# Attention and feed-forward on one core: the ordered list of the work is made by another procedure

## Chip, core and metric

The kernel runs on one core of one Trainium2 chip. The metric is the device time of one execution in microseconds. Before the change the median of 3 runs is 855.63 us (854.58 to 859.22).

## What is computed

```python
# attention: q, k, v are 8 x 8 x 576 x 64 (batch, heads, positions, head size)
scores = scale * np.matmul(q, k.transpose(0, 1, 3, 2))
rel = pos[:, None] - pos[None, :]
mask = (rel >= 0) & (rel < 64)
scores = np.where(mask, scores, -1000000000.0)
scores = scores - np.max(scores, axis=-1, keepdims=True)
attn = np.exp(scores)
attn = attn / (np.sum(attn, axis=-1, keepdims=True) + 1e-09)
x = np.matmul(attn, v)            # then to 4608 tokens x 512
# feed-forward: w_in 512 x 2048, w_out 2048 x 512
h = x @ w_in
out = np.maximum(0.01 * h, h) @ w_out
```

Each position sees itself and the 63 before it. Everything is float32.

## The kernel before, in words

*Units.* The 576 positions of each batch are cut into blocks of 64. A unit is one block with all 8 heads, and two units are a **pair**; there are 36 pairs, 0 to 35. For each pair the scores go to two PSUM banks (S, L284), come to SBUF with the mask (E, `shield_of`, L694, on VectorE; from pair 20 on `copy_of`, L700, on ScalarE), GpSimd takes the maximum over partitions (P, `max_of`, L709), VectorE subtracts it (B, `minus_of`, L716), ScalarE takes the exponent (X, L720), GpSimd sums over partitions (A, `add_of`, L712), and the values follow on TensorE (V, `values_of`, L768). The sums go through four small DMAs and a reciprocal (L723, L731, L744, L756) before `product_of` (L780, VectorE) scales the values. Pairs 0 to 7 belong to a part that is written out by hand.

*Split weights and x.* A float32 product is made of three matmuls: each operand is split into a high half (a rounded copy, by ScalarE) and a low half (what is left, by VectorE: a subtraction). `prep_low` (called `low` before, L1079), `low_of` (L975), the low half of x (`x_low`, L932) and `wide_low` (L1204) are such low halves.

*Four spans of work on TensorE.* (1) A start written out by hand (the string ORDER) up to about 126 us. (2) The first 1536 tokens: 32 steps of a list called `walk`. A step has 12 matmuls of the first layer (`h`, L955) into a PSUM bank, then ScalarE's `leak` (L969) and `high_of` (L972), then `low_of` (L975) on VectorE, and two steps later 12 matmuls of the second layer (`acc`, L964). Two banks, tags o and h, take the first layer's products in turn. (3) Three further stages of 1024 tokens each, with fewer products by sums and differences of blocks: `m` (first layer, L1155) and either `y` (L1175, in the first of the three) or `z` (L1218, in the last two). Their x comes back from DRAM through `x_build` (differences L910, low halves L932), their weights in sums prepared beforehand (`prepare`, L1050: differences `join_of` L1073, low half L1079), and they are loaded by GpSimd's DMA queue (L1139). `combine` (L1207) makes sums of the activations. (4) The attention of pairs 8 to 35 is woven into spans 2 and 3: a **visit** is the scores or the values of one pair between two of TensorE's large products.

*What sets the order.* From the start of span 2, each operation is entered in a list, `plan`, by `op` (L539): its engine, an estimated duration `us`, its predecessors, a rank, a lag after its predecessors, and for DMAs the time to landing. `arrange` (L551) goes through time: it takes the engine that can begin first, and among the operations that are ready there the one of least rank (numbers written out by hand, such as 0.1 for `low_of`, 0.35 or 1.3 for attention). The order so made is the order of each engine's queue. The estimates know nothing of what one engine does to another. TensorE's large products are one fixed chain (`next_main`, L645); only the visits can move in it. The values of pairs 8 to 19 go into the bank of the first layer that is idle at that moment, so they wait for `low_of` of the product before, and the next product waits for their copy (`take_of`, L775). The scores of pairs 10 to 19 and the values of pairs 8 to 19 (`place="guest"`) may stand only behind a first-layer piece or another guest.

Of the kernel before, what the change touches and what calls it, by code (L numbers as in the profile page):

```python
# [4 lines left out]

# [1 line left out]

# [32 lines left out]
LANES = 8  # L40
# [55 lines left out]

HUGE = float(np.array(0x47EFFE00, np.uint32).view(np.float32))
REBIAS = 2.0 ** -112


def flat(t):
# [4 lines left out]
def band_attention_ffn(ctx: ExitStack, tc: tile.TileContext, qk, vW, vL, w_in, w_out, eye_mask, out, outT):  # L106
# [83 lines left out]
    wi, wo, both = [], [], []  # L190
# [68 lines left out]
    xs = {}  # L259
# [196 lines left out]
    acc, sums, due = {}, {}, []  # L456
# [74 lines left out]
    order, late = ORDER.split("|")  # L531
# [19 lines left out]
    def arrange():  # L551
        free, left = dict.fromkeys(("PE", "DVE", "ACT", "POOL", "SP"), 0.0), list(plan)
        waiting = {e: [] for e in free}
        missing, users = {}, {}
        for x in plan:
            missing[x["n"]] = len(x["after"])
            for a in x["after"]:
                users.setdefault(a["n"], []).append(x)
            if not x["after"]:
                waiting[x["engine"]].append((0.0, x))  # L560
        order, landed, last_place = [], [0.0] * LANES, None

        def fits(x):
            return x["place"] != "guest" or last_place in ("host", "guest")

        def begins(ready, x):
            return max(ready, landed[0]) if x["land"] and x["engine"] != "POOL" else ready

        while any(waiting.values()):
            best = None  # L570
            for e, xs in waiting.items():
                if xs:
                    t = max(free[e], min(begins(*y) for y in xs))
                    if best is None or t < best[0]:
                        best = t, e
            t, e = best
            ready_now = [y for y in waiting[e] if begins(*y) <= t]
            r, x = min([y for y in ready_now if fits(y[1])] or ready_now, key=lambda y: (y[1]["rank"], y[1]["n"]))
            if e == "PE":
                last_place = x["place"]  # L580
                if "bank" in x:
                    for y in [y for y in plan if y.get("opens") and "end" not in y][:1]:
                        y["after"].append(x["bank"])
                        missing[y["n"]] += 1
                        users.setdefault(x["bank"]["n"], []).append(y)
            waiting[e] = [y for y in waiting[e] if y[1] is not x]
            free[e] = t + x["us"]
            x["end"] = free[e] + x["land"]
            if x["land"] and e != "POOL":
                landed.pop(0)  # L590
                landed.append(x["end"])
            order.append(x)
            for y in users.get(x["n"], ()):
                missing[y["n"]] -= 1
                if not missing[y["n"]]:
                    at = max(a["end"] + (0.0 if a["engine"] == y["engine"] and not a["land"] else y["lag"]) for a in y["after"])
                    waiting[y["engine"]].append((at, y))
        assert len(order) == len(plan)
        return order

    MM, TWO, ONE, ACTS = 0.2267, 1.05, 0.72, 0.62

    RING, held = 4, {}
# [49 lines left out]
    for name in late.split():  # L653
        kind = name.rstrip("0123456789")
        n = int(name[len(kind) :])
# [4 lines left out]
        engine, us = ("ACT", ACTS) if kind in ("abs", "chi") else ("DVE", ONE)  # L660
# [7 lines left out]
    ready = {f: [weights_of.get(2 * f + i, {}).get("rest") for i in range(2)] for f in range(FT)}  # L668
# [128 lines left out]
    at, summing = {}, []  # L797
# [88 lines left out]

    def x_build(s, n, xt_of, xt_free, x_free):

        STEP, WIDTH = (0.42, 0.27) if s == 2 else (0.5, 0.35)
# [37 lines left out]
        done = []  # L927
        for a, b, after in ((0, 2, got), (2, 3, got), (3, 7, [d, d2, d3, d4])):
            hi = op("ACT", 0.2 + 0.213 * (b - a), lambda a=a, b=b: nc.scalar.copy(x_view(0, a, b), source(a, b)), *after, *x_free, rank=urge, lag=wait)

            def low(a=a, b=b):
                nc.vector.tensor_tensor(x_view(1, a, b), source(a, b), x_view(0, a, b).bitcast(F32), ALU.subtract)  # L932

            done.append(op("DVE", STEP - 0.27 + WIDTH * (b - a), low, hi, rank=urge))
        return done


# [112 lines left out]
    def prepare(n, f, at, hurry, *freed):  # L1050
# [24 lines left out]
        def high():  # L1075
            nc.scalar.copy(prep(0).bitcast(F32R), prep(1))

        def low():
            nc.vector.tensor_tensor(prep(1).bitcast(F32R), prep(1), prep(0), ALU.subtract)  # L1079

        def keep(i):
# [16 lines left out]
        lo = op("DVE", 1.4, low, hi, rank=hurry)  # L1098
# [365 lines left out]
```

## Time and profile before

| what | us |
|---|---|
| median of 3 runs | 855.63 |
| the profiled execution | 856.94 |
| its span on the core | 855.2 |
| TensorE busy in it | 840.5 |
| VectorE / ScalarE / GpSimd busy | 600.4 / 390.6 / 384.0 |

The profile names engines PE (TensorE), DVE (VectorE), ACT (ScalarE), POOL (GpSimd) and SP (SyncE). In a timeline each row has the start, the length, the engine, the line, the operation with its output and inputs, and how many instructions are merged; a bracket at its end gives the idle time of that engine just before, and what ended it. An engine that is idle but not waited for costs nothing, so the rows of TensorE with a bracket are the ones to look for.

### The profile page before, as it was taken

The page shows a single profiled execution, that of the slowest core. Times are in us where ns is not written, and L with a number is a line of the kernel's source. Part 1 is how long each engine was busy: PE and PEld are TensorE (multiplying, and loading weights), DVE is VectorE, ACT ScalarE, POOL GpSimd, SP SyncE. Part 2 cuts the span into 40 slices and gives each one's busy share as a digit, 9 for nine tenths or more (in the row PEclk, how much of TensorE's full clock was granted, in tenths as well). Part 3 has the DMA queues.
Part 4 walks back from the last instruction along what each step waited for, and adds up shares of the span by engine and source line. Part 5 has one row for each costly group of instructions (what it writes and reads, how often), then busy time and mean ns, then how long its engine had stood idle before and what let it go on. Part 6 is the DMA issues. An engine that isn't in the chain of part 4 may idle for free.

```text
span 855.2 us, 16825 instructions
## 1 busy us (share of the span) xinstructions
PE 840.5 (98%) x6778; PEld 686.8 (80%) x6778; DVE 600.4 (70%) x851; ACT 390.6 (46%) x637; POOL 384.0 (45%) x218
## 2 busy tenths in 40 slices
PE   8999999998999999999999999999999999999998
PEld 5787888886887878888888788878888888888886
DVE  7999885545678678656658996487579955546863
ACT  4666555342334365455555443444365423334431
POOL 5322001777777555776787668656111111111110
PEclk9999999999999999999999999999999999999999
DMA  9884856887889859999999999999988986677682
GB/s 330 264 239 145 266 167 231 284 285 231 268 266 356 294 193 293 298 341 311 316 354 337 372 363 337 378 291 258 303 225 240 246 244 199 197 195 194 192 211 94
DMA packets 143117, 226.80 MB, mean 265 GB/s; under 512 B 15552, under 2 KB 66880, under 8 KB 143040
## 3 DMA queue, kind: packets, MB, share of 16 engines
q0 software_dynamic: 51552, 90.18, 37.9%
q10 hardware_dynamic: 51024, 77.31, 27.9%
q1 hardware_dynamic: 40464, 58.24, 21.4%
q8 instruction: 53, 0.87, 0.4%
q14 instruction: 24, 0.20, 0.1%
HBM read 172.52 MB, written 53.06 MB: 264 GB/s over the span
## 4 chain that ended last, share of the span: by engine, by line
PE 84%; DVE 6%; DMA 5%; issue 2%; ACT 1%; POOL 1%; SPq 0%; ACTq 0%; DVEq 0%; POOLq 0%
PE m L1155 26%; PE z L1218 18%; PE y L1175 10%; PE acc L964 6%; PE h L955 6%; PE h L438 5%; PE acc L474 5%; PE s L284 3%; PE o L768 3%; DMA x_rows<-late_n 1%; DMA p<-x_rows 1%; PE o L374 1%; POOL late_o L712 1%; DMA raw<-w_out 1%; DMA late_r<-rows 1%
## 5 line engine op out<-in xcount | busy, mean ns | idle before, releaser
L1155 PE MATMUL m<-pfew,p 128*128 128x512 f32 x720 | 168.6, 390 | 0.6 <-DVE pxa L1164 0.6
L1155 PEld LDWEIGHTS m<-pfew,p 128*128 128x128 f32 x720 | 134.8, 188 | 29.1 <-DVE pxa L1164 1.0
L1164 DVE TENSOR_TENSOR p<-m,pxa 128x512 f32<-128x512 f32 x60 | 41.3, 690 | 54.2 <-PE m L1155 52.1
L964 PE MATMUL acc<-p,gs 128*128 128x512 f32 x324 | 79.1, 393 | 0.0
L1139 POOL DMA_DIRECT2D p<-w_first x42 | 31.7, 755 | 96.6 <-PE m L1155 62.3
L1167 ACT ACTIVATE p<-p 128x512 f32<-128x512 f32 x60 | 37.6, 630 | 80.4 <-DVE p L1164 80.4
L712 POOL PARTITION_ALL_REDUCE late_o<-late_f x20 | 65.6, 3301 | 14.1 <-ACT late_f L720 8.9
L1164 DVE TENSOR_TENSOR pxa<-m,pxa 128x512 f32<-128x512 f32 x60 | 41.4, 690 | 43.2 <-PE m L1155 42.5
L1155 PE MATMUL m<-pxb,p 128*128 128x512 f32 x288 | 71.2, 393 | 0.3 <-ACT p L1167 0.3
L709 POOL PARTITION_ALL_REDUCE g<-late_f x20 | 37.2, 1907 | 75.7 <-DVE late_f L694 73.4
L712 POOL PARTITION_ALL_REDUCE late_o<-late_e x18 | 60.2, 3367 | 23.7 <-issue 18.4
L964 PEld LDWEIGHTS acc<-p,gs 128*128 128x128 f32 x324 | 60.1, 188 | 13.1
L712 POOL PARTITION_ALL_REDUCE late_o<-e x18 | 58.7, 3287 | 26.4 <-ACT e L720 12.8
L1155 PEld LDWEIGHTS m<-pxb,p 128*128 128x128 f32 x288 | 53.4, 188 | 12.6 <-ACT p L1167 0.7
L1218 PE MATMUL z<-gs,p 128*128 128x512 f32 x240 | 57.6, 389 | 0.0
L955 PE MATMUL h<-pxa,p 128*128 128x512 f32 x228 | 55.6, 391 | 0.2 <-ACT late_n L775 0.2
L1218 PEld LDWEIGHTS z<-gs,p 128*128 128x128 f32 x240 | 45.1, 188 | 9.3
L1139 POOL DMA_DIRECT2D p<-w_second x28 | 22.7, 810 | 66.1 <-PE z L1218 37.0
L1218 PE MATMUL z<-third,p 128*128 128x512 f32 x216 | 51.9, 389 | 0.0
L1218 PE MATMUL z<-pxa,p 128*128 128x512 f32 x216 | 51.9, 389 | 0.0
L955 PEld LDWEIGHTS h<-pxa,p 128*128 128x128 f32 x228 | 42.5, 188 | 9.5 <-ACT late_n L775 0.6
L975 DVE TENSOR_TENSOR gs<-h,gs 128x512 fp32r<-128x512 f32 x32 | 22.0, 687 | 38.7 <-ACT gs L972 38.7
(193 smaller groups left out, 1760.6 us busy)
## 6 DMA issues: line engine op xcount, KB each, us to landing
p<-w_first POOLq DMA_DIRECT2D x42, 1024.0 KB, 7.2
p<-w_second POOLq DMA_DIRECT2D x28, 1024.0 KB, 9.3
p<-w_sums POOLq DMA_DIRECT2D x16, 1024.0 KB, 5.6
qk<-qk ACTq DMA_DIRECT2D x26, 512.0 KB, 5.9
pspare<-w_second ACTq DMA_DIRECT2D x16, 512.0 KB, 8.7
w_sums<-pspare ACTq DMA_DIRECT2D x16, 512.0 KB, 6.3
raw<-w_out ACTq DMA_DIRECT2D x15, 512.0 KB, 4.4
raw<-w_in ACTq DMA_DIRECT2D x14, 512.0 KB, 4.0
```

Source lines behind the costliest of these rows:

```text
L438: nc.tensor.matmul(ps, a[:, k, :], b[:, k, part], start=n == 0, stop=n == len(terms) - 1)
L474: nc.tensor.matmul(acc[c, i], a[:, ts], b, start=begin and n == 0, stop=end and n == 2)
L709: nc.gpsimd.partition_all_reduce(most_of(j), e_of(m)[:, j], P, ReduceOp.max)
L712: nc.gpsimd.partition_all_reduce(sum_of(j), e_of(m)[:, j], P, ReduceOp.add)
L955: nc.tensor.matmul(ps, a[:, k, :], b[:, k], start=i == 0, stop=i == len(terms) - 1)
L964: nc.tensor.matmul(acc[c, i], a[:, i * P : (i + 1) * P], b, start=begin and k == 0, stop=n in ends and k == 2)
L1139: nc.gpsimd.dma_start(to, of, max_dma_last_dim=2048)
L1155: nc.tensor.matmul(tiles[b], w[:, 256 * i + 128 * kt : 256 * i + 128 * kt + 128], x_part(OF_X[k], j, kt), start=begin and c == 0, stop=c = ...
L1164: nc.vector.tensor_tensor(to(), tiles[b], x(), ALU.add)
L1167: nc.scalar.activation(to(), to() if b is None else tiles[b], AF.Prelu, alpha=0.01)
L1175: nc.tensor.matmul(tiles[i], a, b, start=f == 0 and k == 0, stop=f == FT - 1 and k == 2)
L1218: nc.tensor.matmul(tiles[b + i], a, x, start=begin and f == 0 and c == 0, stop=f == half - 1 and c == 2, skip_group_check=not begin,)
```

## The change

`arrange` goes, and `arranged` takes its place. What the operations compute stays, and so do the chain of TensorE's products and the bank for the values of pairs 8 to 19. The new procedure has five parts.

- `measure` replaces the estimated durations and times to landing with measured ones, and marks each operation of VectorE that has two inputs in SBUF (`both`) and each reduction of GpSimd (`reduce`).
- `forward` goes through time as `arrange` did, but by a key that is handed to it. A visit to TensorE is put off until it is due, or joins one that has just run. `port_rule` makes an operation with two inputs in SBUF that would begin during a reduction wait until 0.9 us (maximum) or 1.12 us (sum) before the reduction's end.
- `latest` goes backward from TensorE's chain and gives each operation the latest time at which it can begin.
- `candidates` does both 7 times for each of 3 x 6 pairs of a reserve for DMAs and a lead of the visits, with the latest times as the key.
- `walked` goes through each candidate in order with random delays, and the candidate with the earliest end of TensorE is taken.

```diff
+SLACKS = (1.5, 2.0, 2.5)
+AHEAD = (6.0, 8.0, 10.0, 12.0, 15.0, 20.0)
+ROUNDS = 7
+WALKS = 4
+NOISE = 0.05
+STRETCH = 1.1
+ENTER, LEAVE, SIGNAL = 0.12, 0.2, 0.07
+BOTH_SBUF = {
+    "wide_low": 1.22, "combine": 1.22, "whole_of": 1.22, "prep_low": 1.22, "sub": 0.38, "join_of": 0.41, "x_low": None,
...
+def port_rule(x, t, port, held):
+    end = t + x["us"]
+    if x["both"]:
+        held = end = (port[1] if port[0] <= t < port[1] else t) + x["us"]
+    if x["reduce"]:
+        end = max(t, held) + x["us"]
+        port = end - x["us"], end - (0.9 if x["name"] == "max_of" else 1.12)
+    return end, port, held
...
+    def pe_key(x, t):
+        if due is None or not x["visit"]:
+            return x["rank"] if due is None else 1.0
+        return 0.5 if before or due[x["n"]] <= t else 2.0
...
+def candidates(plan):
+    for dma in SLACKS:
+        slack = dict(dma=dma, POOL=POOL_SLACK, other=0.1)
+        for early in AHEAD:
+            order, hosted = forward(plan, {x["n"]: x["rank"] for x in plan}, slack)
+            for n in range(ROUNDS):
+                late = latest(order, hosted, slack)
+                due = early and {x: t - early for x, t in late.items()}
+                order, hosted = forward(plan, late, slack, due)
+                yield order, hosted
+
+
+def arranged(plan):
+    measure(plan)
+    best = None
+    for order, hosted in candidates(plan):
+        mean = sum(walked(order, hosted, NOISE, STRETCH, i) for i in range(WALKS)) / WALKS
+        if best is None or mean < best[0]:
+            best = mean, order
+    return best[1]
...
-    for x in arrange():
+    for x in arranged(plan):
         x["fn"]()
```

(The rest renames `low` to `x_low` and `prep_low`, so that `measure` can tell them apart.) The new code stands ahead, so the line numbers behind `arrange` grow by 185: L975 becomes L1160, L1079 becomes L1264, L1073 becomes L1258, L780 becomes L965, L768 becomes L953.

What moves is seen in the engines' queues. First VectorE's, around the `low_of` (third row from the end, `gs1_82<-h1_10`) that the values of pair 10 wait for. `pspare` is a tile of weights in preparation, `late_n` values to be scaled, `pxa` the x of the third block of tokens, `late_c` the sums, `s12` the scores of pair 12. Before:

```order
L795 TENSOR_TENSOR pxa1_21_2193<-late_n_1764,pxa0_20_2192 128x4x128
L716 TENSOR_TENSOR late_f_1763<-late_f_1763,g_80 128x512
L694 SCALAR_TENSOR_TENSOR e_76<-s12_0_2199,away_75 128x512
L731 RECIPROCAL late_c0_1768<-late_c0_1768 128x8
L694 SCALAR_TENSOR_TENSOR e_76<-s12_1_2200,away_75 128x512
L1079 TENSOR_TENSOR pspare_18_1777<-pspare_18_1777 128x4x256
L975 TENSOR_TENSOR gs1_82<-h1_10_2174,gs1_82 128x512
L780 TENSOR_TENSOR late_n_1764<-late_n_1764,late_r_1765 128x4x2x64
L795 TENSOR_TENSOR pxa1_21_2193<-late_n_1764,pxa0_20_2192 128x4x128
```

The same place in the queue after the change:

```order
L980 TENSOR_TENSOR pxa1_21_2193<-late_n_1763,pxa0_20_2192 128x4x128
L1258 TENSOR_TENSOR pspare_18_1759<-pspare_18_1759 128x256 x2
L916 RECIPROCAL late_c0_1767<-late_c0_1767 128x8
L1264 TENSOR_TENSOR pspare_18_1759<-pspare_18_1759 128x4x256
L1160 TENSOR_TENSOR gs1_82<-h1_10_2172,gs1_82 128x512
L879 SCALAR_TENSOR_TENSOR e_76<-s12_0_2236,away_75 128x512
L879 SCALAR_TENSOR_TENSOR e_76<-s12_1_2237,away_75 128x512
```

The low half of the weights still stands right ahead of `low_of`, but pair 12's scores are read behind it now, and pair 11's subtraction (`late_f`) has gone from this place.

Second, VectorE's queue around the `low_of` of step h2_6, for which the values of pair 18 wait. `p14` and `p15` are weights in preparation, `pxb` x for the next stage. Before:

```order
L1073 TENSOR_TENSOR p14_24_2914<-p14_24_2914 128x256
L975 TENSOR_TENSOR gs0_81<-h2_5_3294,gs0_81 128x512
L731 RECIPROCAL late_c0_1768<-late_c0_1768 128x8
L1073 TENSOR_TENSOR p14_24_2914<-p14_24_2914 128x256 x3
L1079 TENSOR_TENSOR p14_24_2914<-p14_24_2914 128x4x256
L975 TENSOR_TENSOR gs1_82<-h2_6_3333,gs1_82 128x512
```

After:

```order
L1258 TENSOR_TENSOR p15_23_2844<-p15_23_2844 128x256
L1160 TENSOR_TENSOR gs0_81<-h2_5_3288,gs0_81 128x512
L916 RECIPROCAL late_c0_1767<-late_c0_1767 128x8
L965 TENSOR_TENSOR late_n_1763<-late_n_1763,late_r_1764 128x4x2x64
L1160 TENSOR_TENSOR gs1_82<-h2_6_3329,gs1_82 128x512
L1117 TENSOR_TENSOR pxb_27_3374<-p12_25_3049,pxb_27_3374 128x2x256
L1258 TENSOR_TENSOR p14_24_2959<-p14_24_2959 128x256
```

Between the two `low_of` the weights' preparation is gone and the scaling of a pair's values (`product_of`) is there instead.

Third, TensorE's queue around the values of pair 15 (`o15`); `s17` are scores, `h2_0` and `h2_1` first-layer products. Before:

```order
L284 MATMUL s17_1_2917<-qk1_84 64x64
L768 MATMUL o15_2950<-e_76,more_v_73 64x64 x16
L955 MATMUL h2_0_2904<-pxa0_20_2192,pfew_3_85 128x512
L955 MATMUL h2_0_2904<-pxa1_21_2193,pfew_3_85 128x512
L955 MATMUL h2_0_2904<-pxa0_20_2192,pfew_3_85 128x512 x2
```

After:

```order
L1149 MATMUL acc2_3_2829<-p13_15_1545,gs1_82 128x512 x3
L1140 MATMUL h2_1_2977<-pxa0_20_2192,pfew_3_85 128x512
L1140 MATMUL h2_1_2977<-pxa1_21_2193,pfew_3_85 128x512
L1140 MATMUL h2_1_2977<-pxa0_20_2192,pfew_3_85 128x512 x2
L1140 MATMUL h2_1_2977<-pxa1_21_2193,pfew_3_85 128x512
L1140 MATMUL h2_1_2977<-pxa0_20_2192,pfew_3_85 128x512
L953 MATMUL o15_2991<-e_76,more_v_73 64x64 x16
```

The values stood behind scores; now they stand alone, behind half of a first-layer product, one step later in the walk.

More of the change, by code (lines that the diff above doesn't have):

```diff
@@ new lines, in gap, with visiting @@
+def gap(a, x, slack):
+    if a["land"]:
+        return SIGNAL + slack["dma"]
+    if a["engine"] == x["engine"]:
+        return 0.0
+    return SIGNAL + slack.get(a["engine"], slack["other"])
+def visiting(x, before):
+    return x["us"] + (ENTER if x["visit"] and not before else LEAVE if before and not x["visit"] else 0.0)
+def port_rule(x, t, port, held):
+    end = t + x["us"]
+    if x["both"]:
+        held = end = (port[1] if port[0] <= t < port[1] else t) + x["us"]
[3 more added lines that the diff above has]
+    return end, port, held
@@ new lines, in latest @@
+def latest(order, hosted, slack):
+    late, pinned, t, before = {}, {}, 0.0, False
+    for x in order:
+        if x["engine"] == "PE":
+            if not x["visit"]:
+                pinned[x["n"]] = t
+            t += visiting(x, before)
+            before = x["visit"]
+    taken = {e: ([], []) for e in ("DVE", "ACT", "POOL", "SP")}
+    for x in sorted(order, key=lambda x: x["land"] - x["end"]):
+        ends = [late[y["n"]] - gap(x, y, slack) - x["land"] for y in users_of(x, hosted)]
+        if x["n"] in pinned:
+            ends.append(pinned[x["n"]] + x["us"])
+        end = min(ends, default=t + 20.0)
+        if x["engine"] != "PE":
+            begins, stops = taken[x["engine"]]
+            i = bisect_left(begins, end)
+            while i and stops[i - 1] > end - x["us"] + 1e-9 and begins[i - 1] < end - 1e-9:
+                i -= 1
+                end = min(end, begins[i])
+            i = bisect_left(begins, end - x["us"])
+            begins.insert(i, end - x["us"])
+            stops.insert(i, end)
+        late[x["n"]] = end - x["us"]
+    return late
@@ new lines, in walked, with start @@
+def walked(order, hosted, noise=0.0, stretch=1.0, seed=0):
+    r = Random(seed)
+    queues = {}
+    for x in order:
+        queues.setdefault(x["engine"], []).append(x)
+    at, free = dict.fromkeys(queues, 0), dict.fromkeys(queues, 0.0)
+    done, missing = {}, {x["n"]: len(after_of(x, hosted)) for x in order}
+    port, held, before = (0.0, 0.0), 0.0, False
+    head = {}
+    def start(e):
+        if at[e] == len(queues[e]):
+            return None
+        x = queues[e][at[e]]
+        if missing[x["n"]]:
+            return None
+        t = free[e]
+        for a in after_of(x, hosted):
+            t = max(t, done[a["n"]] + (0.0 if a["engine"] == e and not a["land"] else SIGNAL))
+        return t
+    head = {e: start(e) for e in queues}
+    for _ in order:
+        e = min((e for e in head if head[e] is not None), key=lambda e: head[e])
+        t, x = head[e], queues[e][at[e]]
+        y = x if e == "PE" else {**x, "us": x["us"] * (1 + noise * abs(r.gauss(0, 1)))}
+        end = t + y["us"]
+        if e == "PE":
+            end, before = t + visiting(y, before), x["visit"]
+        elif x["both"] or x["reduce"]:
+            end, port, held = port_rule(y, t, port, held)
+        free[e] = end
+        done[x["n"]] = end + (x["land"] * stretch * (1 + 2 * noise * abs(r.gauss(0, 1))) if x["land"] else 0.0)
+        at[e] += 1
+        touched = {e}
+        for y in users_of(x, hosted):
+            missing[y["n"]] -= 1
+            if not missing[y["n"]]:
+                touched.add(y["engine"])
+        for e in touched:
+            head[e] = start(e)
+    return free["PE"]
@@ L548, in bulk @@
         return op("ACT", 0.5, fn, *after, rank=rank, lag=lag, land=land)
[L551 to L599, printed above, removed]
     MM, TWO, ONE, ACTS = 0.2267, 1.05, 0.72, 0.62
```

103 lines of the change are left out of this document (98 added, 5 removed).

## The prediction

> **What bounds the kernel now.** I read the page's busy shares first. TensorE is the engine that sets the time; the other engines matter only where TensorE waits for them.
>
> ```profile
> span 855.2 us, 16825 instructions
> PE 840.5 (98%) x6778; PEld 686.8 (80%) x6778; DVE 600.4 (70%) x851; ACT 390.6 (46%) x637; POOL 384.0 (45%) x218
> ```
>
> The two numbers differ by 14.7 us. That is the first bound: an order of the same instructions can win little more than this. To see where it lies I went through the timeline of TensorE alone, stretch by stretch, and kept the rows with idle time ahead of them (in brackets, with what ended it). Up to 126 us the order is written out by hand and the change leaves it alone, so only later rows count; the last row is from the view by windows (length, busy time of five engines with instruction counts, granted clock, share and rate of the DMA).
>
> ```profile
> 199.07 1.80 PE L768 MATMUL o<-late_e,v 128*64 128x64 f32 x32 [3.69 <-DVE gs L975]
> 200.80 2.54 PE L955 MATMUL h<-pxb,p 128*128 128x512 f32 x6
> ...
> 262.92 1.15 PE L768 MATMUL o<-e,more_v 128*64 128x64 f32 x32 [1.21 <-DVE gs L975]
> ...
> 308.73 1.15 PE L768 MATMUL o<-e,v 128*64 128x64 f32 x32 [1.00 <-DVE gs L975]
> ...
> 484.56 2.98 PE L1175 MATMUL y<-gs,p 128*128 128x512 f32 x12 [0.57 <-issue]
> ...
> 560.63 1.65 PE L1155 MATMUL m<-pxb,p 128*128 128x512 f32 x6 [0.27 <-ACT p L1167]
> ...
> 568.32 1.65 PE L1155 MATMUL m<-pfew,p 128*128 128x512 f32 x6 [0.57 <-DVE pxa L1164]
> ...
> 190.00:205.00 15.00, 11.31 (x129) 9.25 (x129) 8.81 (x11) 4.13 (x8) 10.14 (x5) 0.89 0.75 250
> ```
>
> The idle times add up to 3.69 + 1.21 + 1.00 + 0.57 + 0.27 + 0.57 = 7.3 us. The first has a second price: behind it the values of pair 10 take 1.80 us and half a product 2.54 us, and the granted clock of that window is 0.89. From the chain of waits (start, length, what) come the same things undisturbed, and the price of a visit of attention to TensorE.
>
> ```profile
> 151.18 1.09 PE s L284 x64
> 152.27 2.95 PE acc L964 x12
> 155.22 2.72 PE h L955 x12
> ...
> 387.74 1.08 PE o L768 x32
> ...
> 421.33 2.02 PE o L768 x64
> ...
> 592.72 30.15 PE m L1155 x132
> ...
> 775.18 76.17 PE z L1218 x336
> ```
>
> Twelve large matmuls take 2.72 us (0.227 each), 2.95 right behind a visit, so entering and leaving costs 0.23 us a group of visits. Values take 1.08 us, two sets in a row 2.02. So pair 10's slow clock cost (1.80 - 1.08) + (2.54 - 1.36 - 0.23) = 1.7 us, of which I count 1.6, since rows of the timeline overlap slightly. Together 7.3 + 1.6 = 8.9 us is what the present order loses at places I can name. From 592 us on there is nothing to win: 132 products in 30.15 us are 0.228 each, 336 in 76.17 us are 0.227.
>
> All three long waits are the values waiting for `low_of` (L975), since they go into the idle first-layer bank, which `low_of` reads last. Why it was late, from the timelines of VectorE and GpSimd:
>
> ```profile
> 195.09 3.23 POOL L712 PARTITION_ALL_REDUCE late_o<-late_f  x1 [1.94 <-DVE late_c L731]
> 195.46 2.96 DVE L1079 TENSOR_TENSOR pspare<-pspare 128x1024 fp32r<-128x1024 f32 x1
> 198.34 0.68 DVE L975 TENSOR_TENSOR gs<-h,gs 128x512 fp32r<-128x512 f32 x1
> ...
> 254.82 6.76 POOL L712 PARTITION_ALL_REDUCE late_o<-late_e  x2 [0.62 <-ACT late_e L720]
> 258.77 2.90 DVE L1079 TENSOR_TENSOR pspare<-pspare 128x1024 fp32r<-128x1024 f32 x1 [1.00 <-ACT pspare L1076]
> 261.59 0.68 DVE L780 TENSOR_TENSOR late_n<-late_n,late_r 128x512 f32<-128x512 f32 x1
> 262.19 0.68 DVE L975 TENSOR_TENSOR gs<-h,gs 128x512 fp32r<-128x512 f32 x1
> ...
> 306.41 1.66 DVE L1079 TENSOR_TENSOR p<-p 128x1024 fp32r<-128x1024 f32 x1 [1.55 <-ACT p L1076]
> 308.00 0.68 DVE L975 TENSOR_TENSOR gs<-h,gs 128x512 fp32r<-128x512 f32 x1
> ...
> 562.46 4.32 POOL L712 PARTITION_ALL_REDUCE late_o<-late_e  x1 [2.36 <-issue]
> 563.60 3.27 DVE L1207 TENSOR_TENSOR p<-p 128x1024 f32<-128x1024 f32 x1
> 566.79 1.48 DVE L1164 TENSOR_TENSOR pxa<-m,pxa 128x512 f32<-128x512 f32 x2
> ```
>
> And the group of L1079 (shortest, middle, longest of one, in ns):
>
> ```profile
> L1079 DVE TENSOR_TENSOR pspare<-pspare x12: 1174/1226/2959, 161.3 to 600.5; 128x1024 fp32r<-128x1024 f32 x12
> ```
>
> Each time an operation with two inputs in SBUF (`prep_low`, L1079; at 563 us `combine`, L1207) stands ahead of the needed one in VectorE's queue, and in three of four cases it starts while GpSimd reduces over partitions and takes 2.9 to 3.3 us in place of 1.23. `low_of`, which reads PSUM, is quick (0.68) but must wait its turn.
>
> **The change, part by part.** *Work.* Nothing is added or removed: the instruction counts of each engine, line by line, are the same in both programs. The last 1111 instructions of TensorE are the same in order too. So every term is a wait or a group of visits.
>
> *The three waits for low_of, -7.5.* They cost 3.69 + 1.6 + 1.21 + 1.00 = 7.5 us. In the new order (shown above) `prep_low` is gone from ahead of pair 18's values. For pair 15 it is three places ahead, not two. For pair 10 it still stands right ahead, but the scores of pair 12 now come just before those values, which gives 1.09 us of cover, and no reduction should be running: pair 12's need these scores, and pair 11's scores lie 96 products (22 us) back, where it was 48. So I take all three as gone, and ask what comes in their place. Counted in TensorE's order, three sets of values (pairs 14, 15 and 18) now stand in the middle of a first-layer product without scores ahead of them. There the margin is nil:
>
> ```profile
> 321.90 2.43 PE L955 MATMUL h<-pxa,p 128*128 128x512 f32 x10
> 321.93 0.59 ACT L972 CAST gs<-h 128x512 fp32r<-128x512 f32 x1 [1.97 <-PE acc L964]
> ...
> 322.55 0.69 DVE L975 TENSOR_TENSOR gs<-h,gs 128x512 fp32r<-128x512 f32 x1 [0.90 <-ACT gs L972]
> ```
>
> `low_of` ends at 323.24; half a product after 321.90 is 323.26. Whatever holds VectorE there goes onto TensorE undiminished. Before, such a place cost nothing (pair 19) or 1.00 (pair 18) or 3.69 (pair 10). Ahead of `low_of` at these three now stands `product_of` (L780, 0.68 above), not a 1.23 us operation. Bounds for pairs 10, 14, 15 and 18 are 0 and 1.0 each; I take 0.3, nearest to the short operation and pair 19: +1.2.
>
> *The waits of the later stages, -1.4 + 1.5.* The three are 0.57 + 0.27 + 0.57 = 1.4 us. There the new order sets pairs closer: TensorE's order has 48 products between the scores of pairs 27 and 28, where it had 69, so more of VectorE's work meets GpSimd's. Bounds: 0 (all avoided) to 3.0 (twice what it was); I take 1.5, about the row's own size, because the cause of 563 us is only partly a matter of order.
>
> *Groups of visits, +0.3.* Counted in TensorE's order, 32 groups become 31: -0.23. Eight pairs of values in a row become four: each loses 2 x 1.08 - 2.02 = 0.14, so +0.56.
>
> *GpSimd's own queue.* Loads of weights for the second and third stages stand behind reductions there. Two rows of the view by groups (total, ns of one):
>
> ```profile
> L712 POOL PARTITION_ALL_REDUCE late_o<-late_f x20 | 65.6, 3301 | 14.1 <-ACT late_f L720 8.9 <-issue 2.1 <-DVE late_c L731 1.9
> L709 POOL PARTITION_ALL_REDUCE g<-late_f x20 | 37.2, 1907 | 75.7 <-DVE late_f L694 73.4 <-ACT late_f L700 2.2
> ```
>
> A pair needs 2 x 3.30 + 2 x 1.91 = 10.4 us of it. From the scores of pair 12 to those of pair 17 the new order has 192 products (43.5 us), and with five scores, five values and five groups of visits some 55 us, so 11 us a pair; before it was 234 products, 13 us. GpSimd is nearly full in that burst. I cost it at 0 because values come 72 products (16 us) behind their scores and a pair's maxima and exponents need less; if this cover goes, each microsecond of lag is one of TensorE's.
>
> *Sum.* -7.5 + 1.2 - 1.4 + 1.5 + 0.3 = -5.9 us. The profiled execution took 856.94 us (its span of 855.2 and 1.7 around it), so it would take 851.0. The median of the three runs shown is 1.3 lower, 855.63, which gives 849.7 us.
>
> **A rule of the Trainium skill beside the rows.** In the rows, VectorE's held operation ends 0.1 us behind the reduction (195.46 + 2.96 = 198.42 against 195.09 + 3.23 = 198.32), so with 1.23 us of its own it began 1.1 us before the reduction's recorded end. The Trainium skill, page "SBUF — State Buffer", section "Who interferes with whom", says that the one that starts first holds the shared ports for its whole instruction and the other is blocked fully. By that rule the held operation would have ended 1.1 us later than it did; the trace shows the ports free earlier, and the measurement decides. The new procedure's constants (1.12 for sums) follow the trace.
>
> **Rivals.** (1) *The waits move.* The order is fitted to durations of one execution, and three places have no margin. If pairs 10, 14, 15 and 18 wait 1.0 each and the later stages 3.0: -7.5 + 4.0 - 1.4 + 3.0 + 0.3 = -1.6, 854.0 us. For it: pair 18 waited 1.00 at such a place. Against: the long operations ahead are gone. Chance 0.27.
> (2) *The reduction holds the ports to its end*, the page's rule as a mechanism here: the plan would then hand out 1.1 us too early at each meeting. With the four places and four later meetings one step worse, 849.7 + 8 x 1.1 = 858.5 us. Against it: the row at 195.46. Chance 0.03. It is the rule of the page named above.
> (3) *The second stage waits for its x.* This one ends slower. The last piece of x for it (L932) must follow the scores of pair 27 by way of reductions, four DMAs and a queue on VectorE:
>
> ```profile
> 435.15 1.09 PE s L284 x64
> ...
> 507.26 3.02 DVE L932 TENSOR_TENSOR pfew<-p,pfew 128x256 fp32r<-128x256 f32 x2
> ...
> 537.96 14.97 PE m L1155 x66
> ```
>
> Before, that took from 435.15 to 510.28, 75.1 us, with 28 us to spare. In the new order 288 products (65.3 us), ten visits (10.9) and five groups (1.2) lie between these scores and the stage's first product: 77.4 us. It decides from 2.3 us more than before on. Against it: most of the 75 us was waiting behind less urgent work, which latest times push back. If VectorE's queue lengthens it by a fifth, to 90.1 us, TensorE stands 12.7 us, and with the slow clock's 1.6: 849.7 + 14.3 = 864.0 us. Chance 0.08.
> (4) *Nothing changes*, because the old waits are given back one for one by the burst on GpSimd: 855.6 us. Chance 0.07.
>
> **How the numbers follow.** My forecast has the remaining 0.55: its own range is 847 (all named waits gone: 855.63 - 8.9 + 0.3) to 852. The range 846 to 858 (a microsecond lower, for small waits that I haven't named) leaves out rival 3, most of rival 2 and the outer ends of the rest, together near 0.2. Half a per cent is 4.3 us, about what a measurement of this kernel can tell from no change: faster means below 851.35, slower above 859.9. The forecast lies mostly below (0.50 of 0.55), and rival 1 a little (0.06 of 0.27): faster 0.56. Slower has rival 3 (0.08), some of rival 2 and of 1 and 4 (0.04): 0.12. The same: 0.32.
>
> **What would show it.** Right: in the new profile no idle time over 1.2 us ahead of L953 (the new line of the values), none that brings the clock below 1.00 after 126 us, L1264 (`prep_low`) mostly at 1.23 us, and no wait at the first product of the second stage. Wrong: waits of 1 us and more ahead of the values of pairs 14, 15 or 18 (rival 1), reductions back to back from pair 12 to 17 with exponents late (rival 4), or a gap before the second stage (rival 3).

## The result, and the profile after

The changed kernel is slower: a median of 868.71 us (866.39 to 870.13, 6 runs) against 855.90 (854.58 to 859.22, 6 runs) of the kernel before, a ratio of 1.014 (1.0117 to 1.0164). The profiled execution took 866.39 us. The first rows of its page:

```profile
span 864.6 us, 16834 instructions
PE 844.2 (98%) x6778; PEld 690.4 (80%) x6778; DVE 608.4 (70%) x851; ACT 391.2 (45%) x637; POOL 387.5 (45%) x218
```

The span grew by 9.4 us; TensorE's busy time grew by 3.7, though it does the same instructions: part of the work ran at a lower clock. Here are the rows of TensorE's timeline that have idle time ahead of them, from 126 us on (small ones under 0.3 us left out):

```profile
196.81 1.15 PE L953 MATMUL o<-late_e,v 128*64 128x64 f32 x32 [1.15 <-DVE gs L1160]
...
264.32 1.15 PE L953 MATMUL o<-e,more_v 128*64 128x64 f32 x32 [0.73 <-DVE gs L1160]
...
291.55 3.02 PE L1140 MATMUL h<-pxa,p 128*128 128x512 f32 x12 [0.62 <-ACT late_n L960]
...
441.01 0.36 PE L520 MATMUL s<-qk,qk 64*64 64x64 f32 x3 [2.85 <-DMA qk<-qk]
...
508.96 0.50 PE L1360 MATMUL y<-gs,p 128*128 128x512 f32 x1 [1.29 <-ACT gs L1385]
...
510.22 2.79 PE L1360 MATMUL y<-gs,p 128*128 128x512 f32 x11 [0.76 <-DVE gs L1389]
...
514.03 0.27 PE L520 MATMUL s<-qk,qk 64*64 64x64 f32 x1 [0.76 <-ACT s L871]
...
530.40 0.33 PE L520 MATMUL s<-qk,qk 64*64 64x64 f32 x2 [0.97 <-ACT s L871]
...
548.01 0.88 PE L520 MATMUL s<-qk,qk 64*64 64x64 f32 x3 [2.99 <-ACT s L871]
...
572.56 4.53 PE L1340 MATMUL m<-pfew,p 128*128 128x512 f32 x18 [0.36 <-DVE p L1349]
```

The three values that waited for `low_of` (now L1160) 3.69, 1.21 and 1.00 us wait 1.15, 0.73 and nothing. But behind 430 us there are seven waits in place of three small ones. Four stand ahead of scores (L520): one for the load of q and k, three for the masks that ScalarE must copy into the bank first (`mask_to`, L871). In the kernel before no scores waited for 0.3 us or more there.

Two rows of TensorE, the first product `m` and the first product `z`, cut the span into three pieces. Of the kernel before, then of the changed one:

```profile
345.00 1.38 PE L1155 MATMUL m<-pxb,p 128*128 128x512 f32 x5
...
622.70 0.62 PE L1218 MATMUL z<-gs,p 128*128 128x512 f32 x2
```

```profile
340.12 1.19 PE L1340 MATMUL m<-pxb,p 128*128 128x512 f32 x4
...
631.91 0.84 PE L1403 MATMUL z<-gs,p 128*128 128x512 f32 x3
```

Up to the first `m` the new order wins 345.00 - 340.12 = 4.9 us. From there to the first `z` it takes 291.8 us in place of 277.7, 14.1 more, with the same number of visits (scores of 14 pairs, values of 16). Behind `z` both take 232.5 to 232.7. So -4.9 + 14.1 + 0.2 = +9.4. The views by windows show what the 14.1 are made of; before, then after (length, busy time of TensorE, its weight loads, VectorE, ScalarE and GpSimd with instruction counts, granted clock, DMA share and rate):

```profile
434.00:538.00 104.00, 103.43 (x1028) 84.82 (x1027) 81.00 (x90) 49.84 (x79) 74.20 (x40) 1.00 1.16 353
538.00:623.00 85.00, 84.08 (x594) 68.62 (x593) 54.26 (x74) 35.82 (x63) 42.05 (x26) 1.00 1.08 307
```

```profile
434.00:538.00 104.00, 97.18 (x1016) 79.67 (x1015) 80.74 (x87) 47.41 (x77) 84.49 (x42) 0.98 1.08 314
538.00:623.00 85.00, 81.60 (x656) 66.79 (x655) 53.44 (x77) 37.18 (x66) 47.84 (x28) 0.96 1.09 321
```

The waits between the first `m` and the first `z` add up to 10.2 us (with one of 0.19 that isn't shown), where they were 1.4 before. The clock of 0.98 and 0.96 costs about 0.02 x 104 + 0.04 x 85 = 5.5 us more, an estimate that is good to a microsecond or so, since the clocks are given to two digits. 8.8 + 5.5 = 14.3, which accounts for the 14.1.

The chain of waits of the two kernels says it most plainly (start, length, what). Before, in this stretch it is TensorE almost alone:

```profile
436.24 15.87 PE y L1175 x69
453.20 2.02 PE o L768 x64
455.22 11.81 PE y L1175 x51
```

After, it leaves TensorE again and again:

```profile
420.52 5.21 DMA x_rows<-late_n
425.75 0.53 ACTq L1250
...
426.54 14.34 DMA qk<-qk
...
441.01 1.89 PE s L520 x64
...
538.67 7.02 DMA x_rows<-late_n
545.76 0.56 ACTq L1268
546.37 0.63 ACT late_f L905
...
547.47 1.02 ACT s L871 x2
548.53 1.98 PE s L520 x62
...
555.51 13.42 DMA pspare<-w_second
...
572.56 4.53 PE m L1340 x18
```

Its first break: a load of q and k (`load_qk`, L412), issued at 426.54 just behind two fetches of weights (L1250) on the same queue, takes 14.34 us to land; the second of the fetches had itself been held until a DMA of values landed at 425.73. Its second: ScalarE's queue holds a store of weights (L1268) that may be issued only when an earlier DMA of another queue has landed; behind it stand an exponent and then the masks that the next scores need. ScalarE's own timeline has this as a row (ACTq is its sequencer):

```profile
539.60 6.73 ACTq L1268 DMA_DIRECT2D w_sums<-pspare  x2
546.37 0.63 ACT L905 ACTIVATE late_f<-late_f 128x512 f32<-128x512 f32 x1 [6.25 <-DMA x_rows<-late_n]
```

Why here and not before? In TensorE's order the scores of pairs 22 to 35 stand 51 to 84 products apart before (63.7 on the mean), and 42 to 72 after (51.2). The procedure lets pair 21 run at product 1188, puts pair 22 off to 1356 (it was 1230), and must then place the rest closer. Each pair's load has the scores of the pair before it among its predecessors, so the load, the scores themselves and the queues in between all have to fit into one distance, and 42 products are 9.5 us. How long such a load takes from issue to landing stands in the view of the tile `qk` from 390 to 560 us, before and after:

```profile
DMA to landing us min/median/max: 6.7/9.5/10.9
```

```profile
DMA to landing us min/median/max: 4.2/7.9/14.3
```

The loads are not slower as a rule. There is less room for them.

### The profile page after: what moved, and what is told of

The parts are those of the page before. It is cut to its first block, busy times and chain, and to the rows that moved or that the text cites. A ratio compares the mean times of both kernels' runs of the same rounds, so it can differ in the third digit from the quotient of the medians.

```text
span 864.6 us, 16834 instructions
## 1 busy us (share of the span) xinstructions
PE 844.2 (98%) x6778; PEld 690.4 (80%) x6778; DVE 608.4 (70%) x851; ACT 391.2 (45%) x637; POOL 387.5 (45%) x218
## 4 chain that ended last, share of the span: by engine, by line
PE 78%; DMA 13%; DVE 4%; issue 2%; ACT 1%; SPq 1%; ACTq 1%; DVEq 0%
PE m L1340 24%; PE z L1403 18%; PE h L1140 8%; PE acc L1149 7%; PE h L674 5%; PE acc L710 5%; PE y L1360 4%; PE s L520 3%; PE o L953 3%; DMA pspare<-w_second 3%; DMA x_rows<-late_n 2%; DMA qk<-qk 2%; DMA w_sums<-pspare 2%; DMA w_second<-p 1%; DMA w_first<-p 1%
## 5 line engine op out<-in xcount | busy, mean ns | idle before, releaser
L897 POOL PARTITION_ALL_REDUCE late_o<-late_f x20 | 68.8, 3468 | 16.4 <-ACT late_f L905 6.8
L897 POOL PARTITION_ALL_REDUCE late_o<-e x18 | 60.6, 3404 | 14.7 <-ACT e L905 12.3
L1385 ACT CAST gs<-p 128x1024 fp32r<-128x1024 f32 x27 | 28.5, 1055 | 46.9 <-PE z L1403 21.6
```

Source lines behind the costliest of these rows:

```text
L897: nc.gpsimd.partition_all_reduce(sum_of(j), e_of(m)[:, j], P, ReduceOp.add)
```

## The experiments

The expectations name theories by letters; those that the verdicts use are these. **A**: the loss comes from putting pair 22 off and starting late. **P** (A2 in the first runs): it comes from the distance between pairs, whatever the start. **Q** (B2 in the first runs): it comes from ScalarE's queue, where DMA issues that wait stand ahead of masks and exponents. **K**: it comes from latest times as the key of ScalarE's and VectorE's queues. Where the expectations say "first product of the second stage" they mean the first `m` (340.12 above), and by "first product of the third stage" the first `z`. All kernels issue the operations of the changed one, in other orders or from another queue. The pieces and waits below are those of the profiled execution, the median is that of all runs.

Three of these orders, most reserve and both with loads of 14 us, don't compute the right values for the 128 tokens of pair 19. Its reciprocals stand in a tile (`late_o`) that the sum of pair 20 (`add_of`) writes next, and nothing in the plan makes that sum wait until pair 19's values are scaled (`product_of`). In the kernel before, in the changed one and in the other orders the scaling comes first; in these three the sum does. In the run with 14 us in the later stages, GpSimd's row and then VectorE's:

```profile
319.82 3.21 POOL L897 PARTITION_ALL_REDUCE late_o<-late_f  x1
```

```profile
323.43 0.68 DVE L965 TENSOR_TENSOR late_n<-late_n,late_o 128x512 f32<-128x512 f32 x1
```

The operations are all there, and the place lies ahead of the first `m`, so the times of these three bear on the question, but they are no kernels to use, and what follows does not rest on them alone.

**New, then old.** The new procedure up to the first `m`; from there the old ranks, durations and lags.

```diff
+        if mode and x["name"] == "product" and offset is None:
+            old = mode == "new_old"
+            offset = t - AT_SWITCH if mode == "old_new" else 0.0
+            key = ranks if old else late_key
...
+        us, land = (x["us0"], x["land0"]) if old else (x["us"], x["land"])
```

> The order of the new procedure up to the first product of the second first-layer stage (m), then the old rule: ranks, estimated durations and lags. Theory A (the loss lies in the stages alone, because visits are put off there and then stand too close; the first 32 steps gained): the lag of TensorE at the scores of pair 21 stays as after the change (some 5.5 us less than before), the stages wait as before: 855.9 - 5.5 = 850.4 us, between 849 and 853. Theory B (the loss comes with the new order as a whole, the first part leaves work behind that the stages pay for): 858 us or more.

Measured: 852.38 us (849.56 to 853.06, 5 runs), ratio 0.9933 (0.991 to 0.9957). Its two cuts:

```profile
342.08 1.19 PE L1360 MATMUL m<-pxb,p 128*128 128x512 f32 x4
...
618.76 0.61 PE L1423 MATMUL z<-gs,p 128*128 128x512 f32 x2
```

The second piece is 276.7 us. Theory A's window (849 to 853) holds. Of the 4.9 us won up to the first `m`, 2.9 stay here (4.1 when the same kernel ran again, below), and the loss behind it is gone: it lies in the later stages alone. This version beats both kernels.

**Old, then new.** The same switch the other way round.

> The old rule up to the first product of the m stage, then the new procedure's latest times and its putting off of visits. Theory A: the waits of the first 32 steps come back (5.5 us) and those of the stages stay: 868.7 + 5.5 = 874 us, between 871 and 877. Theory B: the stages lose little behind the old start: 856 to 864 us.

Measured: 872.37 us (868.66 to 873.45, 4 runs), ratio 1.0168 (1.0136 to 1.0201). The total is in theory A's window (871 to 877), but not because two unchanged halves add. The pieces are 350.1 and 288.4 us. The second loses 10.7 us against the kernel before; the first is 5.1 us longer than in it, since its order is not quite the old one (the values of pair 18 come 24 products earlier) and TensorE waits four times for `low_of` (3.18, 1.57, 0.75 and 1.93 us). Again a load of q and k behind two fetches landed in 14.3 us, and TensorE stood 2.88 us for it.

**Late visits at once.** Scores from pair 22 on and values from pair 20 on aren't put off; keys and numbers stay.

```diff
+        if mode == "soon" and x["fn"].args[0] >= (22 if x["name"] == "scores_of" else 20):
+            return 0.5
```

> As after the change, with the same keys, but the scores of pairs 22 to 35 and the values of pairs 20 to 35 aren't put off: they go as soon as they are ready. Theory A: the scores of pair 22 move from 168 products into the stage to about 60, pairs stand closer in the m stage but have room at the end, and the waits of the second-layer stage go: 849 to 855 us. Theory A2 (it is the distance between pairs, 42 to 57 products, whatever the start): the waits move forward into the m stage and stay: 862 to 869 us. Theory B2 (ScalarE's queue: DMA issues that must wait stand ahead of masks and exponents, whatever the visits do): 862 to 869 us, with the waits ended by ScalarE's masks.

Measured: 865.08 us (864.18 to 865.23, 4 runs), ratio 1.0087 (1.0059 to 1.0116). Pair 22 now stands at product 1248, and the pairs after it are still 51.7 products apart on the mean. The second piece is 290.0 us. Theory A falls: starting in time doesn't help when the pairs stay close.

**Most reserve.** Only the largest reserve and the longest lead are offered.

```diff
-SLACKS = (1.5, 2.0, 2.5)
-AHEAD = (6.0, 8.0, 10.0, 12.0, 15.0, 20.0)
+SLACKS = (2.5,)
+AHEAD = (20.0,)
```

> The new procedure held to its largest reserve for DMAs (2.5 us) and its largest lead of visits (20 us) in place of the 1.5 and 6 us that it chose; all else the same. Theory A: the visits start earlier and spread (48 to 78 products between pairs), the waits of the second-layer stage go, and the first 32 steps may wait a little more than after the change: 850 to 857 us. Theory B2: ScalarE's queue still blocks, 862 us or more.

Measured: 864.19 us (861.57 to 872.28, 10 runs), ratio 1.0095 (1.0066 to 1.0123). The pieces are 349.4 and 278.1 us; but this list has scores of one pair and values of two more ahead of the first `m`, about 3.3 us of visits. Counted alike, 346.1 and 281.4: the later stages recover most (58.4 products apart on the mean), while the first piece loses what it had won. The total misses A's window (850 to 857) and lies in Q's (862 or more), but it doesn't separate the theories, since both pieces move.

**Even pace.** From pair 22 on, scores are let onto TensorE 15.5 us after the scores before.

```diff
+        if mode and x["name"] == "scores_of" and x["fn"].args[0] >= 22:
+            return 0.5 if t >= mode + paced[0] else 2.0
```

> From pair 22 on, scores are let onto TensorE 15.5 us after the scores of the pair before (57 to 66 products between most pairs, where the changed kernel has 42 to 72); the keys of all other engines stay the latest times of the chosen list. Theory P (the later stages lose because pairs follow each other in 42 to 54 products, about 13 us, and the load of q and k, which may start only when the scores before it have read its buffer, takes 8 to 14 us): 849 to 855. Theory Q (ScalarE's queue: DMA issues that wait stand ahead of masks and exponents): 858 to 866, since the order on that queue is much the same. Theory K (latest times as keys for ScalarE and VectorE are what costs, whatever the distance of the pairs): 860 to 868.

Measured: 855.83 us (851.03 to 862.3, 10 runs), ratio 0.9985 (0.9956 to 1.0015): a microsecond above P's window, far below Q's and K's. The second piece is 278.3 us with every other key a latest time. What is left are two waits over a microsecond, both for VectorE (the low half of `y`'s operand, `wide_low`, and the sum behind `m`):

```profile
515.93 2.79 PE L1369 MATMUL y<-pxa,p 128*128 128x512 f32 x11 [1.70 <-DVE pxa L1398]
...
559.44 0.73 PE L1349 MATMUL m<-pxb,p 128*128 128x512 f32 x2 [1.23 <-DVE p L1358]
```

**Old ranks, new numbers.** Behind the first `m` the old ranks choose, but with the new durations, lags and lock. Against the first experiment (the lags, the price of a visit and the lock change in further lines, not shown):

```diff
             key = ranks if old else late_key
-        us, land = (x["us0"], x["land0"]) if old else (x["us"], x["land"])
+        us, land = x["us"], x["land"]
```

> The changed kernel's list up to the first product of the second stage; behind it the old ranks choose on every engine, visits without due times, but with the new procedure's durations, lags and lock. Pairs 22 to 29 follow in 42 to 54 products. Theory P (distance of the pairs): 858 to 868, with waits for loads of q and k or for sums, though every key is the old one. Theory K (the keys): 849 to 854, as the run that kept old ranks with old numbers. Theory Q (ScalarE's queue): 852 to 862, not sharp.

Measured: 859.11 us (854.71 to 864.37, 10 runs), ratio 1.0016 (0.9992 to 1.0041). K's window (849 to 854) is missed: the old keys alone, with pairs 54.9 products apart, are 6.7 us slower than with the old numbers. P's holds. Q's held too, so this run doesn't separate those two. The second piece is 280.5 us in the profiled execution, which at 854.87 was one of the two shortest of the ten; the first of its waits is one for the scaling of values (L983):

```profile
385.85 1.15 PE L971 MATMUL o<-late_f,more_v 128*64 128x64 f32 x32 [1.45 <-DVE late_n L983]
```

**Loads reckoned at 14 us.** One number of the table.

```diff
-            x["land"] = 2.8 if x["land"] < 5 else (5.0 if x["land"] < 6.6 else 7.5)
+            x["land"] = 2.8 if x["land"] < 5 else (5.0 if x["land"] < 6.6 else 7.5 if name == "load_v" else 14.0)
```

> The changed kernel with one number of its table changed: a load of q and k is reckoned at 14 us to its landing (the longest seen where two fetches of the weights stand ahead of it on the queue) in place of 7.5. The procedure then puts pairs 22 to 35 at 66 to 84 products from each other and starts on pair 22 at product 1176 in place of 1356. Theory P: 847 to 855. Theory K: 860 to 868, keys being latest times as before. Theory Q: 856 to 866.

Measured: 862.18 us (857.42 to 862.82, 6 runs), ratio 1.0044 (1.0027 to 1.0061). A miss for P by the total, which lies in K's and Q's windows. The profiled execution, with 857.42 us the shortest of the six by 4 us, has pieces of 348.5 and 274.4 us, with the same 3.3 us of visits moved ahead as above: counted alike 345.2 and 277.7. In this execution the later stages are as in the kernel before, as P says; where the other five lost 4 to 5 us more isn't recorded. The number also spoiled the first piece, which I had not reckoned with: the list that came to be chosen is another one from early on (scores of pair 20 at product 1002, where the changed kernel has 1050).

**Weights on SyncE's queue.** The order stays; only the queue that issues the fetches and stores of the weights changes.

```diff
-                nc.scalar.dma_start(to, w_second[:, f::half, 512 * i : 512 * (i + 1)])
+                nc.sync.dma_start(to, w_second[:, f::half, 512 * i : 512 * (i + 1)])
...
-                nc.scalar.dma_start(w_sums[:, :, f, 256 * i : 256 * (i + 1)], prep(i))
+                nc.sync.dma_start(w_sums[:, :, f, 256 * i : 256 * (i + 1)], prep(i))
```

> The changed kernel's order, every instruction in its place; only the fetches of the second weights and the stores of their sums are issued from SyncE's queue instead of ScalarE's. Theory Q (their waits hold up masks and exponents on ScalarE): 852 to 858. Theory P: 860 to 870; the load of pair 26 may land sooner without two fetches ahead of it on its queue (then its wait of 2.9 us goes, about -4 us with the slow clock behind it), but the pairs still follow each other in 42 to 54 products. Theory K: 864 to 870.

Measured: 865.81 us (864.14 to 866.57, 4 runs), ratio 1.0085 (1.0064 to 1.0107). Q's window (852 to 858) is missed; P's and K's both hold. The second piece is 290.3 us. The wait for pair 26's load shrank from 2.85 to 0.40 us, but a larger one came up at another place:

```profile
439.25 0.36 PE L520 MATMUL s<-qk,qk 64*64 64x64 f32 x3 [0.40 <-DMA qk<-qk]
...
554.85 2.93 PE L1340 MATMUL m<-pxb,p 128*128 128x512 f32 x6 [4.36 <-ACT p L1352]
```

So clearing those two kinds of issues from ScalarE's queue wins 1.5 us of the 14.1 in the profiled executions (by the ratios of the medians, 1.0085 against 1.014, about 5). The 4.36 us wait hangs on ScalarE once more: its queue held a load of values (issued at 553.78) until a DMA of SyncE's queue, 8.24 us from issue to landing, had landed. ScalarE's queue as a whole is therefore not cleared of blame by this run. The Trainium skill, page "Trainium Kernel Development and Optimization", section "Key Constraints", says that DMAs issued from the different queues share the same 16 DMA engines, and that several issuers save only issue time. The run agrees in its sum (290.3 against 291.8 us): with the two fetches on the other queue, pair 26's load, issued at 426.79, still took some 12.4 us (the scores that waited for it start at 439.25), where it had taken 14.34.

**14 us in the later stages only**, with reserve and lead held at 1.5 and 6.0.

```diff
-            x["land"] = 2.8 if x["land"] < 5 else (5.0 if x["land"] < 6.6 else 7.5)
+            x["land"] = 2.8 if x["land"] < 5 else (5.0 if x["land"] < 6.6 else 14.0 if name == "load_qk" and f.args[0] >= 22 else 7.5)
```

> As the run with 14 us for every load, but only the loads of pairs 22 to 35 are reckoned at 14 us, and reserve and lead are held at those of the changed kernel's list (1.5 and 6.0), so that its first 21 pairs stand where they stand there (scores of pair 21 at product 1188). Pairs 22 to 35 follow each other in 63 to 81 products. Theory P (distance of the pairs): the second stage's first product at 340 to 343 us as in the changed kernel, 277 to 280 us from there to the first product of the third stage as in the kernel before, 850 to 855 in all. Theory K (latest times as keys): 288 us or more between those two, 862 to 870 in all.

Measured: 856.63 us (852.36 to 865.23, 12 runs), ratio 0.9988 (0.9967 to 1.001); the profiled execution 854.59. Its second piece:

```profile
342.80 0.73 PE L1340 MATMUL m<-pxb,p 128*128 128x512 f32 x2
...
619.99 0.39 PE L1403 MATMUL z<-gs,p 128*128 128x512 f32 x1
```

342.8 and 277.2 us, both as P has them, with latest times as keys, as in the run with an even pace: K falls here too. The median is 1.6 us above the window, while the profiled execution lies in it. This list brought back a wait for `low_of` in the first piece; what share of the 1.6 us that has isn't shown:

```profile
306.72 1.15 PE L953 MATMUL o<-e,v 128*64 128x64 f32 x32 [2.88 <-DVE gs L1160]
```

**A pace of 12.5 us.** The even pace with one constant changed.

```diff
-MODE = 15.5
+MODE = 12.5
```

> The even pace again, with 12.5 us in place of 15.5 as the shortest time from scores to scores (42 to 60 products between most pairs); nothing else differs from that run. Theory P: the second stage and the rest up to the third stage's first product take 285 to 291 us again, where the 15.5 us pace had 278.3; 860 to 868 in all. If instead the start on pair 22 at product 1356 was what cost (theory A), it stays at 278 to 280 and 854 to 858 in all.

Measured: 865.17 us (862.57 to 873.5, 5 runs), ratio 1.0109 (1.0067 to 1.015). The second piece is 285.6 us, 7.3 more than with 15.5 us. The total and the piece are in P's windows (860 to 868, 285 to 291), and outside A's. The same kinds of waits are back:

```profile
417.09 1.50 PE L962 MATMUL o<-late_e,more_v 128*64 128x64 f32 x32 [2.22 <-DMA more_v<-vL]
...
472.77 0.33 PE L529 MATMUL s<-qk,qk 64*64 64x64 f32 x2 [1.01 <-ACT s L880]
```

This is the cleanest pair of runs, and both orders compute the right values: the one constant sets the distance, and the loss follows it.

**New, then old, again**, unchanged.

> The first experiment's kernel once more, unchanged, beside the run with 14 us loads in the stages: 850 to 854 by every theory; it says which of the two is the shorter and how far the chips agree.

Measured: 851.58 us (850.0 to 855.07, 6 runs), ratio 0.9929 (0.9904 to 0.9953), as the first time (0.9933). It is the best of the study.

All kernels, in the order of the mean distance of pairs 22 to 35. "From m to z" is the profiled execution's second piece; in the two marked *, 3.3 us are moved to it from the first piece, for the visits that those lists make ahead of the first `m`. For "old ranks, new numbers" and "14 us for all loads" the profiled execution is over 4 us shorter than the median, so their pieces are at the low end.

| kernel | products between pairs | to first m, us | from m to z, us | ratio |
|---|---|---|---|---|
| old, then new | 50.8 | 350.1 | 288.4 | 1.0168 |
| the changed kernel | 51.2 | 340.1 | 291.8 | 1.014 |
| weights on SyncE | 51.2 | 340.8 | 290.3 | 1.0085 |
| late visits at once | 51.7 | 340.9 | 290.0 | 1.0087 |
| pace of 12.5 us | 53.1 | 342.5 | 285.6 | 1.0109 |
| old ranks, new numbers | 54.9 | 340.1 | 280.5 | 1.0016 |
| most reserve | 58.4 | 346.1* | 281.4* | 1.0095 |
| even pace, 15.5 us | 59.1 | 343.3 | 278.3 | 0.9985 |
| new, then old (both runs) | 59.5 | 342.1, 340.9 | 276.7, 276.5 | 0.9933, 0.9929 |
| the kernel before | 63.7 | 345.0 | 277.7 | 1 |
| 14 us in the later stages | 69.2 | 342.8 | 277.2 | 0.9988 |
| 14 us for all loads | 74.8 | 345.2* | 277.7* | 1.0044 |

Under 55 products the second piece grows quickly; over some 59 it is flat at about 277 us, close to what the products and visits need (an estimate from the prices in the prediction: 1056 products of 0.227 us, 14 scores of 1.09, 16 values at 1.08 or two at 2.02, and 16 groups of visits at 0.23 make 275 us).

## Why the prediction was wrong, by its own steps

The forecast was 849.7 us; the median came out at 868.71, the other way from 855.63.

*The three waits for low_of, -7.5 + 1.2.* The mechanism was right, and the size nearly: up to the first `m` the sum said about -6 with the groups of visits, and 4.9 us were won. Pair 18 doesn't wait any more, and pair 10's wait no longer slows the clock (1.00 from 190 to 205 us). Of the four places without a margin two waited, pair 10 for 1.15 and pair 15 for 0.73 us, 1.9 in all where 1.2 stood; the copy of values out of the bank added 0.62. One count in the groups of visits was off: seven pairs of values stood in a row, not eight, so that term is +0.2 in place of +0.3. Pair 10's was not the lock. VectorE's timeline:

```profile
194.93 1.23 DVE L1264 TENSOR_TENSOR pspare<-pspare 128x1024 fp32r<-128x1024 f32 x1 [1.00 <-ACT pspare L1261]
196.07 0.68 DVE L1160 TENSOR_TENSOR gs<-h,gs 128x512 fp32r<-128x512 f32 x1
```

`prep_low` takes its undisturbed 1.23 us, as forecast, but starts late because it waits 1.00 us for ScalarE's rounding, and `low_of` stands behind it. Over the kernel three of its sixteen take clearly longer, the longest 2596 ns:

```profile
L1264 DVE TENSOR_TENSOR pspare<-pspare x12: 1207/1221/2596, 165.0 to 604.7; 128x1024 fp32r<-128x1024 f32 x12
```

*GpSimd's own queue, costed at 0.* Right for the burst from pair 12 to 17, where TensorE waited for `low_of` (0.73 us) and for the copy of values (0.62 us), but for no pair's exponents. For the later stages I hadn't costed it at all. A pair needs two sums and two maxima, by the groups of the page

```profile
L897 POOL PARTITION_ALL_REDUCE late_o<-late_f x20 | 68.8, 3468 | 16.4 <-ACT late_f L905 6.8
L894 POOL PARTITION_ALL_REDUCE g<-late_f x20 | 37.0, 1883 | 79.2 <-DVE late_f L879 70.6
```

2 x 3.47 + 2 x 1.88 = 10.7 us, and with the loads of weights it issues GpSimd was 84.49 us of 104 busy, where it was 74.20.

*The waits of the later stages, -1.4 + 1.5.* **This is the step that failed.** It measured -1.4 + 10.2, and 5.5 for the clock: 14.1 us more than before in place of 0.1. I had seen the cause, 48 products between pairs 27 and 28 where there had been 69, and gave it a bound of 3.0 us as if only VectorE's meetings with GpSimd could grow. What I left out was the chain of each pair, from its load to its exponents, that must fit into that distance. Its first link was in the profile of before, 6.7 to 10.9 us from issue to landing, on a queue that is shared with the weights' transfers. A list with 42 products (9.5 us) and a visit or two between scores has nothing left over for that. The plan reckoned 7.5 us for the load, and with a reserve of 1.5 us believed it could.

*Rivals.* None of them named this. Rival 3, the only slow one, did not happen: the second `m` block starts behind the last `y` without a wait. Rival 1 (waits of 1.0 at four places, 3.0 in the stages) had the right place for its second half, at a third of its waits. Rival 2, the ports held to the reduction's end, isn't borne out. One `prep_low` was held by a sum again; VectorE's row, then GpSimd's:

```profile
258.22 2.29 DVE L1264 TENSOR_TENSOR pspare<-pspare 128x1024 fp32r<-128x1024 f32 x1 [0.26 <-ACT pspare L1261]
```

```profile
257.11 3.31 POOL L897 PARTITION_ALL_REDUCE late_o<-late_e  x1
```

It ends at 260.51, 0.1 behind the sum's 260.42, so with 1.22 us of its own it began 1.1 us ahead of that recorded end, as the procedure's constant has it.

*What is shown and what stays open.* That the loss lies between the first `m` and the first `z` is shown by the two switched kernels; that the distance of the pairs sets it, by the two paces; the loads of 14 us in the later stages agree, in an order that computes pair 19 wrongly. Which link gives way first isn't settled. The load, ScalarE's queue behind a DMA issue that waits, and GpSimd are all tight at 12 to 13 us a pair, and moving the weights to SyncE's queue only let another wait come up, on ScalarE's queue again. Whether a distance of 51 products would do with shorter landing times wasn't tried. Nor is it excluded that latest times as keys make a short distance dearer: "late visits at once" and "old ranks, new numbers" both have three distances of 42 products, and the second, with the old ranks and a mean of 54.9 in place of 51.7, took 9.5 us less from `m` to `z`. Nor did any run separate what the measured durations, the lock and the latest times each bring in the first piece.

## What to carry to other kernels

When an order is made anew, look not only at the waits that it removes but at how close it sets repeated chains, and compare that distance with the sum of the chain's links as the profile of before shows them under load, transfers foremost. An old order's even rhythm can be a reserve that no rule states: here 59 products and more between pairs cost nothing, and 51 cost 14 us. A new order also lays bare what the plan never said: an old one can respect a dependence that no predecessor states, as pair 20's sum behind pair 19's scaling. And where a new procedure helps one part and harms another, try it on each part alone; the half that helped was worth 0.7% by itself.

## What the runs showed of the hardware that I had not expected

A load of 512 KB that was issued 2.5 us behind the first of two fetches of 512 KB on the same queue landed in 14.3 us, once in each of two kernels (the changed one, and old, then new). The shared queue is no full explanation: with the two fetches on another queue the load still took some 12.4 us. Another load of the changed kernel took 13.5 us; it was issued at 499.1 us, over 7 us after the last transfer before it on its queue, but a store issued there at 490.3 took 12.7 us to land and so was still under way. And an engine that issues a DMA can be held there until a DMA of another engine's queue has landed: 6.73 us in ScalarE's queue for two issues, during which the exponents behind them could not start.
